# v's block rows in one transfer per pair, whole halo rows without clears, and a new order of the work

## The chip, the cores and the metric

The kernel runs on one core of one Trainium2 chip. The metric is the device time of one execution in microseconds: the median of three runs is 269.15 us (268.91 to 269.34). A core has five engines with queues of their own: TensorE (PE, matmuls), VectorE (DVE), ScalarE (ACT), GpSimd (POOL) and SyncE (SP, which here only issues DMA transfers).

## The reference

Attention over a window of 16 keys to either side plus 24 block summaries (the maximum of k and the mean of v over 32 rows), a value projection with a convolved gate, and a spatial-gating MLP. B, H, S, D are 2, 8, 768, 64; the model width is 512, w_in is 512 x 1024, w_spatial 768 x 768. Cut to what matters:

```python
k_sum = k.reshape(B, H, nb, block, D).max(axis=3)
v_sum = v.reshape(B, H, nb, block, D).mean(axis=3)
mask_l = np.abs(pos[:, None] - pos[None, :]) < window
scores_s = scale * np.einsum('bhsd,bhnd->bhsn', q, k_sum) + np.log(block)
scores_all = np.concatenate([np.where(mask_l, scale * q @ kT, -1e9), scores_s], axis=-1)
attn = softmax(scores_all) @ np.concatenate([v, v_sum], axis=2)        # then x = heads side by side
gate_pre += conv_w[k][None, None, :] * xp[:, k:k + S, :]               # k = 0..4
x = (sigmoid(gate_pre) * (x @ w_val)) @ w_out
u, v = halves of np.maximum(x @ w_in, 0.0)
v_s = np.einsum('ts,bsd->btd', w_spatial, normalised v) + b_spatial[None, :, None]
out = (u * v_s) @ w_out2
```

## The kernel before, in words

Nothing is issued where it is written. Every operation is recorded by the class Planner (record, L100), given a duration by cost (L161), and put in order by plan (L232): a list scheduler that keeps each engine's free time, the slots of 33 tiles of 128 x 1536 floats and of 8 PSUM banks, and a model of the DMA queue. Whatever is ready first goes first; among what is ready within LOOK (L43) of that, the priority decides, which is the place in ORDER (L45). All instructions are then issued by issue (L214), so the trace gives each of them line 230; nearly all tiles in SBUF are called at_u, all PSUM banks at_ps. DMA transfers for SP share 8 semaphores, and the transfer n waits for the landing of transfer n - 8.

ORDER is a list of tokens; each calls the next step of a piece (step, L1276), and a step that needs another calls it first (need, L1286). The pieces that count here:

- mask and hot: the masks and the identity (moves) made by POOL, and awake (L586), nine filler matmuls of moves by moves.
- wout, in1, in0, wval: the loads of w_out, the two halves of w_in, and w_val (split64 L571, load64 L553). The weights are float64 in DRAM; a block of 128 x 512 comes as 512 KB, ACT and DVE (a shift and an or) assemble float32 from it. cw (conv_weights L593) does the same with the 20 KB of convolution weights, which POOL's own queue loads, and POOL copies them to the tile cw.
- wp (w_product L1199): the product of w_out and w_in, 32 matmuls of 128 x 512, first the half n = 1 from in1 and then the half n = 0 from in0, four to a step.
- lk, lq, lv: loads of k, q, v for a pair of heads (L611, L606, L632); kw (windows L616) builds keys in windows and takes the block maximum km on DVE. Pairs 0 to 3 are the first batch, 4 to 7 the second.
- vsum (reduce_v L647) loads v once more in rows and adds up the means on DVE; put (put_vsum L665) sends them by four small SP transfers of 24 x 128 to the partitions 96 to 119, and POOL copies them into the pair's v tile.
- score (L680), at (a_T L712) and pv (L726): for a pair and half of the sequence the 24 score matmuls, the masked maximum on DVE (six operations), the exponential on ACT, the scaling on POOL, six transposes on PE, and 24 matmuls with v; pv also starts the convolution on DVE.
- gate, val0/1, u0/1, v0/1, s0/1, f0/1, ws, out2, r: the projections and the spatial gating, whose products are of 128 x 384 and whose operands are split in two rounded parts by ACT and POOL.

The v tile of a pair holds for each of 12 blocks of 64 queries, and for 2 heads, 120 rows: 32 to 95 are the block itself, 0 to 31 the 16 rows before and the 16 after it, interleaved, 96 to 119 the means. The rows outside the sequence's ends carry weight zero, since the mask puts -1e9 there. In load_v (L632) POOL clears the 32 halo rows of the first and last block, and four SP transfers bring two halves of the 64 rows and the halo rows, shifted by one block.

Of the kernel before, what the change touches and what calls it, by code (L numbers as in the profile page):

```python
# [18 lines left out]
WK = 96  # L19
# [23 lines left out]
LOOK = {"PE": 0, "ACT": 0, "DVE": 0, "POOL": 100, "SP": 200}  # L43

ORDER = """  # L45
    mask in1 hot mask hot wout*2 in1 hot*4 in1 wval wout in1 lk lq hot wval wout lk wp lk wp hot lk kw*2 in0*2 score
    wp lq*2 in0 score kw vsum wp lq in0 vsum score kw score lv score wp*2 at put cw pv lv put score wp at pv lv
    wval*2 put at score*2 wp lv*2 at lk put hot lk at vsum lv at*2 pv*2 kw gate lq lv lq kw wu lq pv*2 val0 wu
    val0*2 lk at wv val0 lv pv wu pv wu wv lk score*2 kw u0 kw u0 gate val0 wv val0 wv vsum u0 put score*2 put lq
    score*4 val0 at u0 v0 at val0 v0 at*2 pv*4 at put v0 at*2 v0*2 put at pv*3 gate pv gate v0 f0 u0 ws*2 val1*4 f0  # L50
    val1 s0 val1 u0 v1 val1 v1 ws u1 v1 ws val1 u0 s0 u1 f1 f0 v1*2 s0 f0 v1 s0 out2 u1 u0 u1 f1 ws f1 s0*2 f1 u1 s0
    s1 out2 f0 s0 s1 s0 out2 ws u1 f0 u1 s1 s0 ws f0 u1 out2 s1*2 s0 s1 s0*2 r*2 s0 r f1*2 s1 r*2 s1 r s1*4 f1 s1*2
    r*6
"""

WIN = 10240 / 3
# [9 lines left out]
class Planner:  # L66
# [86 lines left out]
    @staticmethod  # L153
    def size(ap):
        n = 1
        for _, c in ap.ap[1:]:
            n *= c
        return n

    @staticmethod  # L160
    def cost(o, eng, method, args, kw, ins, outs):  # L161

        size = Planner.size
        n = max(size(x) for x in ins + outs)
        if eng == "PE":
            rhs = args[2]
            cols = size(rhs) if method == "matmul" else args[1].ap[0][1]
            if method == "transpose":
                return 109, None, 0, False
            if rhs.dtype == F32 and outs[0].ap[0][1] > 64:  # L170
                return 4 * cols / 2.4 + 8, None, 0, False
            if rhs.dtype == F32:
                return (4 * cols / (6 if cols > 64 else 4.8) + 8), None, 0, False
            return (cols / 2.4 + 14 if rhs.dtype != BF16 else 200 if cols > 16 else 80), None, 0, False
        psum = any(x.tensor.name.startswith("ps") for x in ins)
        if method == "dma_start":
            run = 4 * min(outs[0].ap[-1][1], ins[0].ap[-1][1]) if ins else 512
            total = 4 * size(outs[0]) * outs[0].ap[0][1]
            parts = outs[0].ap[0][1]
            o.rate = next(k for k in range(16, 0, -1) if parts % k == 0)  # L180
            rate = 130 if run <= 512 else 405 if parts > 96 else 235 if parts > 64 else 380 if parts > 16 else 210
            return (600 if eng == "POOL" else 840 if len(outs[0].ap) > 2 else 600 if parts == 64 else 410), None, total / rate, False
        if eng == "ACT":
            ptr = sum(1 for k in ("bias", "scale") if hasattr(kw.get(k), "ap")) + (method == "mul" and hasattr(args[2], "ap"))
            func = args[2] if method == "activation" else None
            if n <= 4 and outs[0].tensor.name.startswith("ps"):
                return 200, None, 0, False
            table = {AF.Exp: "exp", AF.Tanh: "exp", AF.Prelu: "exp"}.get(func)
            return (n + (61 if psum else 112)) / 1.2 + 93 * ptr + (92 if "accum_out" in kw else 0) + 45 * (func == AF.Prelu), table, 0, False
        sbuf_in = [x for x in ins if not x.tensor.name.startswith("ps")]  # L190
        big = [x for x in sbuf_in if size(x) > 1]
        if eng == "DVE":
            out_psum = outs[0].tensor.name.startswith("ps")
            if method == "memset":
                return n / 0.96, None, 0, False
            one = method in ("tensor_copy", "tensor_scalar") and not psum and not out_psum
            lock = one or len(big) > 1 or n == 1 and not psum
            ptr = sum(1 for x in args[2:5] if hasattr(x, "ap") and size(x) == 1) if method != "tensor_tensor" else 0
            if method == "tensor_reduce" and ins[0].ap[-1][0] > 32:
                n = 1.75 * n  # L200
            per = 8 * n if method == "reciprocal" else n / 2 if one else n
            return (per + 66) / 0.96 + 58 * ptr + 9 * (method == "tensor_tensor_reduce"), None, 0, lock
        if method == "memset":
            return n / 1.2 + 30, None, 0, False
        if method == "affine_select":
            return 450, None, 0, True
        two = len(big) > 1
        if n == 1:
            return 550, None, 0, True
        if two and ins[-1].ap[-1][0] == 0:  # L210
            return 790, None, 0, True
        return (2.45 if two else 1.1 if method == "tensor_copy" else 2.85) * n / 1.2 + 190, None, 0, True
# [237 lines left out]
def tile_kernel(ctx, tc, q, k, v, vn, w_val, conv_w, w_out, w_in, w_sp, b_sp, w_out2, mask_l, mask_r, eye, out):  # L450
    nc = tc.nc
    B, H, S, D = vn.shape
    DM = H * D
    NP = H // 2
    NB = S // QB
# [4 lines left out]
    pe, act, dve, pool, sp = plan.PE, plan.ACT, plan.DVE, plan.POOL, plan.SP  # L460
# [12 lines left out]
    def unit(dt=F32R, n=1536, kind=0):  # L473
        uid[0] += 1
        x = homes.tile([P, 1536], dt, tag="h0", name=f"u{uid[0]}", bufs=1)
        return plan.tile(x, "u", NU, (kind, n))[:, :n]
# [20 lines left out]
    def cst(shape, dt, name):  # L497
        return plan.tile(const.tile(shape, dt, name=name), "const " + name, 1)
# [92 lines left out]
    cw = cst([P, KT, 5], F32, "cw")  # L591
# [11 lines left out]
    QT, KT_, KWT, VW, vsum = {}, {}, {}, {}, {}  # L603
# [28 lines left out]
    def load_v(n):  # L632
        b, p = pairs[n]
        vw = VW[n] = unit(F32).rearrange("p (h j d) -> p h j d", h=2, d=D)
        pool.memset(vw[0:32, :, 0 :: NB - 1, :], 0.0)

        src, dst = v[b, p], vw.rearrange("p h j d -> p (h j d)")
        for h in range(2):
            sp.dma_start(dst[32:WK, h * NB * D : (h + 1) * NB * D], src[:, h * NB * D : (h + 1) * NB * D])
        sp.dma_start(dst[0:32:2, D:], src[48:64, :-D])  # L640
        sp.dma_start(dst[1:32:2, :-D], src[0:16, D:])

    rows = vn.rearrange("b h (n k) d -> (b h n) (k d)", k=32)
    stage, MS, MEAN = Parts(4 * 2 * D, F32), {}, {}
# [599 lines left out]
    def each(n, piece):  # L1244
# [4 lines left out]
    NG = len(ticks)  # L1249
    threads = {  # L1250
        "lk": each(NPR, load_k), "lq": each(NPR, load_q), "mask": load_masks(), "hot": each(9, awake), "kw": each(NPR, windows), "lv": each(NPR, load_v),
        "vsum": each(4, reduce_v), "put": each(NPR, put_vsum), "cw": conv_weights(),
        "score": each(NG, scores), "at": each(NG, a_T), "pv": each(NG, pv), "gate": each(B * NC, gate),
# [122 lines left out]
```

## Time and profile before

| | |
|---|---|
| median of three runs | 269.15 us |
| profiled execution: its own time | 269.44 us |
| profiled execution: span of its instructions | 267.7 us |
| PE busy | 255.7 us, 96% |
| DVE busy | 189.3 us, 71% |
| ACT busy | 158.1 us, 59% |
| POOL busy | 164.1 us, 61% |
| moved by DMA | 31.73 MB, mean 119 GB/s |
| chain that ended last | PE 73%, DMA 17%, SP's queue 3%, POOL 3%, ACT 2%, DVE 1% |

The page comes from one profiled execution. A busy PE is a modelled time, since matmuls are pipelined. The chain is followed back from the last instruction to whatever released each step. In a timeline, consecutive instructions of one kind are put together with a count, and the bracket says how long the engine idled ahead of them and what ended that.

### The profile page before, as it was taken

Reading aid. Unit: us, or ns where it says so; the run is one execution under the profiler, and the core shown is the slowest. Engines: PE = TensorE matmul, PEld = TensorE weight load, DVE = VectorE, ACT = ScalarE, POOL = GpSimd, SP = SyncE. Lnnn points to the kernel's source line nnn. Section 1 sums busy time; section 2 is a strip of 40 time slices with the busy share of each in tenths; the row PEclk is TensorE's granted clock in tenths of the full one; section 3 lists DMA queues with packets and bytes.
Section 4 is the critical chain, followed back from the end, with each engine's and each line's share of the span. In section 5 each row is a group of like instructions: output and inputs, shape, how many; then the busy total and the mean of one; then the engine's idle time right before and its main releaser. Section 6 shows DMA issues by size and latency. Waiting matters only on the chain.

```text
span 267.7 us, 5433 instructions
## 1 busy us (share of the span) xinstructions
PE 255.7 (96%) x1882; PEld 220.7 (82%) x1882; DVE 189.3 (71%) x558; ACT 158.1 (59%) x440; POOL 164.1 (61%) x197
## 2 busy tenths in 40 slices
PE   7799999869999999999999999999999999999995
PEld 5245655459999998988999899889999898889884
DVE  1778998569989995799986868947975547308200
ACT  2459996977998999957570206153445734423311
POOL 6047328475989546991856507586299599684500
PEclk9999999997999999999999999999999999999999
DMA  6999989599761002440000000002004200321122
GB/s 225 390 406 406 400 236 281 156 320 242 291 165 48 2 4 68 147 149 2 5 0 0 0 2 0 0 0 78 4 1 159 43 36 0 115 83 39 42 101 95
DMA packets 11291, 31.73 MB, mean 119 GB/s; under 512 B 1648, under 2 KB 2112, under 8 KB 11264
## 3 DMA queue, kind: packets, MB, share of 16 engines
q1 hardware_dynamic: 11232, 31.37, 34.6%
q8 instruction: 15, 0.25, 0.4%
q14 instruction: 12, 0.10, 0.1%
q0 software_dynamic: 32, 0.02, 0.0%
HBM read 28.14 MB, written 3.15 MB: 117 GB/s over the span
## 4 chain that ended last, share of the span: by engine, by line
PE 73%; DMA 17%; SPq 3%; POOL 3%; ACT 2%; DVE 1%; issue 1%; DVEq 0%; ACTq 0%
PE at_ps L230 73%; DMA at_u<-in_moe_w_out_dram 6%; DMA at_u<-in_k_dram 5%; DMA at_u<-in_q_dram 4%; SPq L230 3%; POOL at_u L230 3%; DMA at_u<-in_moe_w_val_dram 2%; ACT at_u L230 2%; DVE at_u L230 0%; DVE km L230 0%; ACT at_ps L230 0%; DVEq L230 0%; ACTq L230 0%
## 5 line engine op out<-in xcount | busy, mean ns | idle before, releaser
L230 PE MATMUL at_ps<-at_u,at_u 128*128 128x384 f32 (+4 forms) x1752 | 233.5, 323 | 4.0 <-ACT at_u L230 2.1
L230 PEld LDWEIGHTS at_ps<-at_u,at_u 128*128 128x128 f32 (+2 forms) x1752 | 202.4, 190 | 31.6 <-issue 11.6
L230 POOL TENSOR_TENSOR at_u<-at_u,at_u 128x384 fp32r<-128x384 f32 (+2 forms) x83 | 102.8, 1261 | 53.1 <-ACT at_u L230 50.9
L230 ACT CAST at_u<-at_u 128x384 fp32r<-128x384 f32 (+2 forms) x83 | 45.3, 589 | 32.1 <-DVE at_u L230 26.7
L230 ACT COPY at_u<-at_ps 120x384 f32<-120x384 f32 (+3 forms) x61 | 28.0, 500 | 32.9 <-PE at_ps L230 32.5
L230 POOL TENSOR_TENSOR at_u<-at_u,sm 128x360 f32<-128x360 f32 x32 | 25.1, 814 | 18.9 <-ACT at_u L230 9.5
L230 ACT ACTIVATE at_u<-at_u,nm 128x120 f32<-128x120 f32 x96 | 36.5, 389 | 0.3 <-DVE nm L230 0.3
L230 DVE SCALAR_TENSOR_TENSOR at_u<-at_ps,cw,at_u 128x384 f32<-128x384 f32 (+4 forms) x64 | 36.3, 610 | 0.0
L230 DVE TENSOR_TENSOR at_u<-at_ps,at_u 128x384 f32<-128x384 f32 (+1 forms) x36 | 19.8, 554 | 22.7 <-PE at_ps L230 20.7
L230 ACT ACTIVATE at_ps<-at_u 128x512 f32<-128x512 f32 x20 | 13.0, 652 | 20.7 <-DMA at_u<-in_moe_w_out_dram 11.4
L230 DVE CUSTOM_DVE_ANT_0 at_u<-at_ps,mask 128x120 f32<-128x120 f32 x96 | 21.3, 273 | 0.4 <-PE at_ps L230 0.3
L230 DVE TENSOR_TENSOR at_u<-at_u,at_u 128x256 f32<-128x256 f32 (+2 forms) x25 | 19.8, 793 | 1.3 <-PE at_ps L230 0.7
L230 ACT ACTIVATE at_u<-at_ps 128x512 f32<-128x512 f32 x20 | 11.6, 596 | 14.2 <-PE at_ps L230 14.1
L230 POOL COPY at_u<-at_u 128x320 f32<-128x320 f32 (+2 forms) x24 | 18.1, 772 | 1.7 <-DMA at_u<-at_u 1.2
L230 ACT ACTIVATION_READ_ACCUMULATOR at_u<-at_u,nm 128x1 f32 x96 | 18.6, 194 | 0.0
L230 DVE TENSOR_SCALAR at_u<-at_u 128x512 uint32<-128x512 uint32 (+1 forms) x21 | 11.5, 547 | 9.3 <-DMA at_u<-in_moe_w_in_dram 5.6
L230 DVE TENSOR_TENSOR at_u<-at_u 128x384 f32<-128x384 f32 (+5 forms) x31 | 16.2, 534 | 2.6 <-PE at_ps L230 2.6
L230 DVE SCALAR_TENSOR_TENSOR at_u<-at_ps,at_u 128x512 uint32<-128x512 uint32 x20 | 13.8, 690 | 3.8 <-ACT at_ps L230 2.2
L230 PE MATMUL at_ps<-moves,at_u 128*120 128x128 f32 x96 | 12.9, 274 | 2.2 <-DVE at_u L230 2.2
L230 PEld LDWEIGHTS at_ps<-moves,at_u 128*120 128x120 f32 x96 | 11.0, 137 | 4.4 <-DVE at_u L230 2.4
L230 POOL TENSOR_TENSOR va<-va,power 128x1 f32<-128x1 f32 x12 | 8.0, 667 | 10.1 <-DVE va L230 10.1
L230 DVE BATCH_NORM_STATS2 st<-at_u 128x6 f32<-128x512 f32 x12 | 8.2, 688 | 7.3 <-ACT at_u L230 7.3
(38 smaller groups left out, 138.1 us busy)
## 6 DMA issues: line engine op xcount, KB each, us to landing
at_u<-in_moe_w_in_dram SPq DMA_DIRECT2D x8, 512.0 KB, 8.3
at_u<-in_moe_w_out_dram SPq DMA_DIRECT2D x8, 512.0 KB, 6.3
at_u<-in_k_dram SPq DMA_DIRECT2D x8, 384.0 KB, 7.6
at_u<-in_q_dram SPq DMA_DIRECT2D x8, 384.0 KB, 6.9
at_u<-in_vn_dram SPq DMA_DIRECT2D x6, 512.0 KB, 9.1
at_u<-in_v_dram SPq DMA_DIRECT2D x16, 192.0 KB, 5.4
out_dram<-at_u SPq DMA_DIRECT2D x11, 256.0 KB, 2.0
at_u<-in_moe_w_spatial_dram SPq DMA_DIRECT2D x6, 384.0 KB, 3.6
```

The source lines that it names most:

```text
L230: getattr(real, method)(*[home(x) for x in args], **{k: home(x) for k, x in kw.items()})
```

## The change

load_v no longer clears the halo rows. It brings the 64 block rows of both heads by one transfer of 64 x 1536, and the halo rows by two transfers of 16 x 1536 whose source starts one block of a head earlier or later (D elements to the left or to the right), so that the rows are whole; the ends now hold values of neighbouring rows in place of zeros. In Planner.cost the rates of small transfers and one issue time change. ORDER is another list; of it only the first lines are shown.

```diff
 ORDER = """
-    mask in1 hot mask hot wout*2 in1 hot*4 in1 wval wout in1 lk lq hot wval wout lk wp lk wp hot lk kw*2 in0*2 score
-    wp lq*2 in0 score kw vsum wp lq in0 vsum score kw score lv score wp*2 at put cw pv lv put score wp at pv lv
...
+    mask hot wout hot in1*2 hot wout hot*2 lk in1 lq mask hot kw lk wout hot cw wp in0 lq lk score wout in0 in1 hot
+    wp kw lq score kw wp*2 lk kw in0 hot in0 vsum score wp wval at lq lv vsum put at score*2 wv lv wval put pv*2 lv
...
@@ Planner.cost, dma_start
-            rate = 130 if run <= 512 else 405 if parts > 96 else 235 if parts > 64 else 380 if parts > 16 else 210
-            return (600 if eng == "POOL" else 840 if len(outs[0].ap) > 2 else 600 if parts == 64 else 410), None, total / rate, False
+            rate = 130 if run <= 512 else 405 if parts > 96 else 235 if parts > 64 else 260 if parts > 16 else 150
+            return (600 if eng == "POOL" else 980 if parts < 32 and run <= 512 else 840 if len(outs[0].ap) > 2 else 600 if parts == 64 else 410), None, total / rate, False
@@ load_v
         vw = VW[n] = unit(F32).rearrange("p (h j d) -> p h j d", h=2, d=D)
-        pool.memset(vw[0:32, :, 0 :: NB - 1, :], 0.0)
-
         src, dst = v[b, p], vw.rearrange("p h j d -> p (h j d)")
-        for h in range(2):
-            sp.dma_start(dst[32:WK, h * NB * D : (h + 1) * NB * D], src[:, h * NB * D : (h + 1) * NB * D])
-        sp.dma_start(dst[0:32:2, D:], src[48:64, :-D])
-        sp.dma_start(dst[1:32:2, :-D], src[0:16, D:])
+        sp.dma_start(dst[32:WK], src)
+
+        n = 2 * NB * D
+        for t, at in ((0, 48 * n - D), (1, D)):
+            sp.dma_start(dst[t:32:2], bass.AP(src.tensor, src.offset + at, [[n, 16], [1, n]]))
```

What the new list does to the engines, at three places.

The first place is DVE at the very start. An operation TENSOR_SCALAR of 128x512 with the SCALAR_TENSOR_TENSOR behind it assembles one block of a weight; those of 128x20 do the same for the convolution weights. Before:

```order
L230 TENSOR_SCALAR at_u_74_708<-at_u_74_708 128x512
L230 SCALAR_TENSOR_TENSOR at_u_73_771<-at_ps_75_756,at_u_74_708 128x512
L230 TENSOR_SCALAR at_u_79_711<-at_u_79_711 128x512
L230 SCALAR_TENSOR_TENSOR at_u_73_771<-at_ps_80_769,at_u_79_711 128x512
L230 TENSOR_SCALAR at_u_82_718<-at_u_82_718 128x512
L230 SCALAR_TENSOR_TENSOR at_u_73_771<-at_ps_83_781,at_u_82_718 128x512
L230 TENSOR_SCALAR at_u_85_723<-at_u_85_723 128x512
L230 SCALAR_TENSOR_TENSOR at_u_84_793<-at_ps_86_789,at_u_85_723 128x512
```

With the change:

```order
L230 TENSOR_SCALAR at_u_75_708<-at_u_75_708 128x512
L230 SCALAR_TENSOR_TENSOR at_u_74_767<-at_ps_76_754,at_u_75_708 128x512
L230 TENSOR_SCALAR at_u_103_711<-at_u_103_711 128x20
L230 SCALAR_TENSOR_TENSOR at_u_103_711<-at_u_103_711 128x20
L230 TENSOR_SCALAR at_u_79_713<-at_u_79_713 128x512
L230 SCALAR_TENSOR_TENSOR at_u_74_767<-at_ps_80_775,at_u_79_713 128x512
L230 TENSOR_SCALAR at_u_82_717<-at_u_82_717 128x512
L230 SCALAR_TENSOR_TENSOR at_u_74_767<-at_ps_83_785,at_u_82_717 128x512
```

The first block is now one of w_out, and the two operations on the convolution weights stand behind it, ahead of the first block of w_in. They stood far behind these rows before.

The second place is SP's list in the stretch of v. in_v_dram is v by blocks (lv), in_vn_dram v by rows (vsum), the 24x128 transfers are the means (put), and the last in_k_dram rows are k of the pairs 4 and 5. Before, with pair 0's four transfers of v right ahead of the first row:

```order
L230 DMA at_u_204_922<-in_v_dram 64x768 x2
L230 DMA at_u_204_922<-in_v_dram 16x1472 x2
L230 DMA at_u_221_932<-in_v_dram 64x768 x2
L230 DMA at_u_221_932<-in_v_dram 16x1472 x2
L230 DMA at_u_222_1110<-in_moe_w_val_dram 128x1024
L230 DMA at_u_226_1113<-in_moe_w_val_dram 128x1024
L230 DMA at_u_250_1095<-in_v_dram 64x768 x2
L230 DMA at_u_250_1095<-in_v_dram 16x1472 x2
L230 DMA at_u_251_1106<-in_v_dram 64x768 x2
L230 DMA at_u_198_1171<-at_u_155_1104 24x128 x4
L230 DMA at_u_251_1106<-in_v_dram 16x1472 x2
L230 DMA at_u_256_1240<-in_k_dram 128x768 x2
```

With the change, with three transfers each of the pairs 0 and 1 not far ahead:

```order
L230 DMA at_u_202_1041<-in_moe_w_val_dram 128x1024
L230 DMA at_u_213_1055<-in_v_dram 64x1536
L230 DMA at_u_213_1055<-in_v_dram 16x1536 x2
L230 DMA at_u_214_1110<-in_v_dram 64x1536
L230 DMA at_u_214_1110<-in_v_dram 16x1536 x2
L230 DMA at_u_215_1137<-in_moe_w_val_dram 128x1024
L230 DMA at_u_242_1162<-in_q_dram 128x768
L230 DMA at_u_180_1194<-at_u_158_1064 24x128 x4
L230 DMA at_u_247_1228<-in_moe_w_val_dram 128x1024
L230 DMA at_u_251_1232<-in_k_dram 128x768
L230 DMA at_u_242_1162<-in_q_dram 128x768
L230 DMA at_u_251_1232<-in_k_dram 128x768
```

Before, k of the pairs 4 and 5 stands behind five pairs of v with four transfers each; now behind four pairs with three, and behind one q more. The loads of w_val that stood third and sixth in the whole list before now stand among the v rows.

The third place is DVE around the block maxima of the pairs 4 and 5 (TENSOR_REDUCE km). The 128x512 rows are the last blocks of w_val, the rows with cw the convolution of the first pv. Before:

```order
L230 TENSOR_REDUCE km_282<-at_u_256_1240 128x24
L230 TENSOR_REDUCE km_287<-at_u_256_1240 128x24
L230 TENSOR_SCALAR at_u_226_1113<-at_u_226_1113 128x512
L230 SCALAR_TENSOR_TENSOR at_u_226_1113<-at_ps_227_1202,at_u_226_1113 128x512
L230 TENSOR_TENSOR at_u_201_1313<-at_ps_200_1290,at_u_201_1313 128x384
L230 SCALAR_TENSOR_TENSOR at_u_203_1323<-at_ps_200_1290,cw,at_u_203_1323 128x383
L230 SCALAR_TENSOR_TENSOR at_u_203_1323<-at_ps_200_1290,cw,at_u_203_1323 128x382
L230 TENSOR_TENSOR at_u_201_1313<-at_ps_218_1325,at_u_201_1313 128x384
```

With the change:

```order
L230 TENSOR_REDUCE km_289<-at_u_251_1232 128x24
L230 TENSOR_SCALAR at_u_247_1228<-at_u_247_1228 128x512
L230 SCALAR_TENSOR_TENSOR at_u_247_1228<-at_ps_248_1295,at_u_247_1228 128x512
L230 TENSOR_TENSOR at_u_207_1324<-at_ps_206_1300,at_u_207_1324 128x384
L230 SCALAR_TENSOR_TENSOR at_u_209_1332<-at_ps_206_1300,cw,at_u_209_1332 128x383
L230 TENSOR_REDUCE km_305<-at_u_251_1232 128x24
L230 SCALAR_TENSOR_TENSOR at_u_209_1332<-at_ps_206_1300,cw,at_u_209_1332 128x382
L230 TENSOR_TENSOR at_u_207_1324<-at_ps_210_1330,at_u_207_1324 128x384
```

The second maximum moved from ahead of the w_val block to behind it and behind the first two operations of pair 0's pv.

## Rows read from the trace of the kernel before

**Rows 1.** The page, part 1: busy time, share of the span, instructions.

```profile
PE 255.7 (96%) x1882; PEld 220.7 (82%) x1882; DVE 189.3 (71%) x558; ACT 158.1 (59%) x440; POOL 164.1 (61%) x197
```

**Rows 2.** Timeline of PE, 195 to 268 us.

```profile
210.96 53.68 PE L230 MATMUL at_ps<-at_u,at_u 128*128 128x384 f32 x273 [0.60 <-ACT at_u L230]
```

**Rows 3.** Timeline of PE, 0 to 70 us: start, us, engine, line, what, [idle before <-releaser].

```profile
1.87 5.46 PE L230 MATMUL at_ps<-moves 128*128 128x264 f32 x14 [1.87 <-POOL moves L230]
8.25 1.95 PE L230 MATMUL at_ps<-at_u 128*128 128x512 f32 x4 [0.92 <-DVE at_u L230]
...
16.53 0.61 PE L230 MATMUL at_ps<-moves 128*128 128x264 f32 x2
...
22.72 3.70 PE L230 MATMUL at_ps<-at_u 128*128 128x512 f32 x8
26.35 5.85 PE L230 MATMUL at_ps<-at_u,at_u 64*64 64x120 f32 x78
32.77 3.98 PE L230 MATMUL at_ps<-at_u,at_u 64*64 64x120 f32 x30 [0.58 <-DMA at_u<-in_q_dram]
...
47.09 1.88 PE L230 MATMUL at_ps<-at_u,at_u 64*64 64x120 f32 x44 [0.90 <-ACT at_u L230]
49.61 3.70 PE L230 MATMUL at_ps<-at_u,at_u 128*128 128x512 f32 x8 [0.63 <-ACT at_u L230]
53.50 0.99 PE L230 MATMUL at_ps<-at_u,at_u 120*64 120x64 f32 x24 [0.19 <-POOL at_u L230]
...
59.28 1.20 PE L230 MATMUL at_ps<-moves,at_u 128*120 128x128 f32 x9 [2.18 <-DVE at_u L230]
```

**Rows 4.** Windows: busy us (count) of PE, PEld, DVE, ACT, POOL, PEclk, DMA share, GB/s.

```profile
60.00:66.00 6.00, 6.00 (x107) 5.76 (x106) 5.96 (x16) 5.28 (x13) 3.02 (x4) 0.72 1.01 246
62.00:64.00 2.00, 2.00 (x44) 2.00 (x42) 2.00 (x6) 1.75 (x7) 0.00 (x0) 0.50 1.02 251
```

**Rows 5.** Groups by line and form, POOL: count, busy us, mean ns.

```profile
L230 POOL MEMSET at_u<- 32x256 f32 x8 | 2.4, 302 | 0.1
```

**Rows 6.** Timeline of SP's queue, 26 to 60 us.

```profile
26.89 14.18 SPq L230 DMA_DIRECT2D at_u<-in_v_dram  x12
```

**Rows 7.** The page, part 2: GB/s in 40 slices of 6.7 us.

```profile
GB/s 225 390 406 406 400 236 281 156 320 242 291 165 48 2 4 68 147 149 2 5 0 0 0 2 0 0 0 78 4 1 159 43 36 0 115 83 39 42 101 95
```

**Rows 8.** Timeline of DVE, 40 to 64 us.

```profile
43.94 0.81 DVE L230 SCALAR_TENSOR_TENSOR at_u<-at_u 128x20 uint32<-128x20 uint32 x1
...
55.22 0.95 DVE L230 TENSOR_REDUCE km<-at_u 128x24 f32<-128x768 f32 x1 [4.34 <-DMA at_u<-in_k_dram]
...
58.53 0.69 DVE L230 SCALAR_TENSOR_TENSOR at_u<-at_ps,at_u 128x512 uint32<-128x512 uint32 x1
```

**Rows 9.** The tile of v's loads: SP's issues, min/median/max ns.

```profile
L230 SPq DMA_DIRECT2D at_u<-in_v_dram x32: 517/536/1367, 26.9 to 74.2; - x32
```

**Rows 10.** Timeline of POOL, 0 to 30 us.

```profile
1.77 0.15 POOL L230 MEMSET mask<- 128x72 f32 x1
```

**Rows 11.** DMA issues: count, KB each, median us to landing.

```profile
at_u<-in_moe_conv_w_dram POOLq DMA_DIRECT2D x1, 20.0 KB, 5.6
```

**Rows 12.** Timeline of DVE, 0 to 13 us.

```profile
10.53 0.69 DVE L230 SCALAR_TENSOR_TENSOR at_u<-at_ps,at_u 128x512 uint32<-128x512 uint32 x1 [0.32 <-ACT at_ps L230]
11.14 0.42 DVE L230 TENSOR_SCALAR at_u<-at_u 128x512 uint32<-128x512 uint32 x1
11.77 0.69 DVE L230 SCALAR_TENSOR_TENSOR at_u<-at_ps,at_u 128x512 uint32<-128x512 uint32 x1 [0.21 <-ACT at_ps L230]
```

**Rows 13.** Groups by line and form, PE and DVE.

```profile
L230 DVE CUSTOM_DVE_ANT_0 at_u<-at_ps,mask 128x120 f32<-128x120 f32 x96 | 21.3, 273 | 0.4 <-PE at_ps L230 0.3
...
L230 PE MATMUL at_ps<-at_u,at_u 64*64 64x120 f32 x384 | 17.7, 303 | 1.5 <-ACT at_u L230 0.9 <-DMA at_u<-in_q_dram 0.6
...
L230 PE MATMUL at_ps<-moves,at_u 128*120 128x128 f32 x96 | 12.9, 274 | 2.2 <-DVE at_u L230 2.2
...
L230 DVE TENSOR_REDUCE km<-at_u 128x24 f32<-128x768 f32 x8 | 7.4, 948 | 5.7 <-DMA at_u<-in_k_dram 5.6
```

More of the change, by code (lines that the diff above doesn't have):

```diff
@@ L45 @@
 ORDER = """
-    mask in1 hot mask hot wout*2 in1 hot*4 in1 wval wout in1 lk lq hot wval wout lk wp lk wp hot lk kw*2 in0*2 score
-    wp lq*2 in0 score kw vsum wp lq in0 vsum score kw score lv score wp*2 at put cw pv lv put score wp at pv lv
[L48 to L53, printed above, removed]
+    mask hot wout hot in1*2 hot wout hot*2 lk in1 lq mask hot kw lk wout hot cw wp in0 lq lk score wout in0 in1 hot
+    wp kw lq score kw wp*2 lk kw in0 hot in0 vsum score wp wval at lq lv vsum put at score*2 wv lv wval put pv*2 lv
+    put lv wval wp at score pv score put lq at wval lk pv wu gate score wp lq wp at lk at lq lk val0 at val0 kw pv
+    val0 at val0 lv wu kw lk kw wv score pv*3 wu lv gate lq score wu vsum u0 kw u0 val0 u0 vsum wv*2 lv at val0
+    put*2 val0 score*6 lv v0 at val0 at v0 u0 at pv*3 at put at v0*2 at*2 pv*3 put pv gate pv ws gate u0 v0*2 val1*2
+    ws f0 val1*2 f0 val1*2 s0 v1 out2 v1 u0 v1 val1*2 u1 ws u1 v1 f1 u1 v1 u1 s1 v1 f0 s0 f1 f0 s1 u1*2 f1 s1 s0 s1
+    s0 f1 u1 f1 ws s0*2 u1 s0 ws s0 s1*2 u0 ws f0*2 s0 out2 s0 out2*2 u0 r s0 s1*2 r s0 f0 ws s0 r s0 r s1*2 f1 s1
+    f1 s1 r s1 r*4 s1 r*3
 """
```

## The prediction

> **What bounds the kernel now.** I read the page's first part, then the timeline of TensorE (PE) with the idle time that ends each stretch, then for each idle time the timeline of the engine it names, and SP's issues last. TensorE is busy for 255.7 of 267.7 us [rows 1], so all its idle time is 12.0 us, and only the places where that stands can give anything. From about 60 us on there is one wait, of 0.60 us [rows 2]; the rest lies ahead. The reader is to see three groups in the timeline [rows 3]: the start (1.87 us until the filler matrix is made, and 0.92 until VectorE, DVE, has assembled the first w_in block), four waits between 32 and 54 us (0.58 + 0.90 + 0.63 + 0.19 = 2.30 us), and 2.18 us ahead of the stretch at 59.28. The last has a tail: the mean granted clock of the 6 us behind it is 0.72, and 0.50 in their middle [rows 4], the lower of the two levels (1.2 GHz). That costs 6 x 0.28 = 1.7 us.
>
> **Time base.** The profiled execution took 269.44 us, 0.29 over the median of 269.15. The sum is made against 269.44, and 0.29 is taken off at the end. About 0.2% (0.54 us) is what a measurement of this kernel can tell from no change.
>
> **The change, part by part.**
>
> *The clears.* Eight POOL memsets of 0.302 us go [rows 5], 2.4 us in all. The transfer of v into the same tile comes behind each of them and hides it, and no engine waits for POOL's clears in the trace: I cost them at nothing. Without that cover they would be worth 2.4 us at most.
>
> *v's transfers.* Two halves of 192 KB become one of 384 KB, and two of 92 KB become two of 96 KB: 576 KB a pair in three issues instead of 568 KB in four, so eight of SP's issues go. In the v stretch SP spent 14.18 us on 12 issues, 1.18 us each [rows 6], and the rate falls from 400 GB/s to 236, 281 and 156 there [rows 7]: the queue did not wait for bytes. No row shows a transfer of 16 x 1536 or 64 x 1536. By bytes at 400 GB/s a pair takes 1.5 us, by issues at 1.18 us it takes 3.5; I take the issues, since v was served at their pace.
>
> *k of the second batch.* It stands in SP's list behind 20 v issues before and behind 12 now, with nearly the same bytes ahead (16.6 and 16.4 MB, added up from the list) and one q load more among them. Before, the first pair's k (pair 4) lands at 55.2, when DVE has idled for 4.34 us [rows 8]. Eight issues of 0.54 us (the median of v's issues [rows 9]) less 0.97 us for the q (0.39 MB at 406 GB/s [rows 7]) are 3.3 us; half of that is my lower value. So it lands between 52 and 53.5.
>
> *The conv weights.* Their POOL transfer moves from the middle of the start to right behind the second memset of the mask at 1.77 us [rows 10], and their two DVE operations come to stand between the first w_out block and the first w_in block. The transfer took 5.6 us to land [rows 11], in a queue as full as the one at the start, so it lands at 1.92 + 5.6 = 7.5. The two operations take some 0.95 (the longer alone 0.81 [rows 8]), the block behind them 1.1 [rows 12], and the first product begins at about 9.75 in place of 8.25: TensorE idles for 2.4 us instead of 0.92. That is 1.5 us; the bounds are nothing (it has landed before DVE comes to it) and 7.1 us (it takes twice 5.6 us).
>
> *The products.* DVE is then the bound: eight blocks at 1.24 us from one to the next [rows 12], three block maxima of k at 0.95, twelve score operations at 0.22 (21.3 / 96) [rows 13], and an estimated 0.6 for four small ones, are 16.0 us behind 9.6. So the last four products of the first half start at 25.6 and, with 3.63 us for four [rows 3], end at 29.25. Before, they end at 26.35, but two scores (1.11 us each: 17.7 over 16 [rows 13]) and a filler (0.61 [rows 3]) fewer have been done by then: like for like, 29.2. So the late start is paid for by the order that follows. From there to the first output matmuls at 53.50, before loses 2.30 us to the four waits. In the new order the work to that point, four sets of 3.63, five scores and four and a half transposes (0.81 each: 12.9 over 16 [rows 13]), runs to 53.0, with 1.2 us of transposes and one filler more behind it than before. **First term: 2.30 - 0.05 = 2.2 us gained**, between 0.8 (the two longest of these waits come back, 0.90 and 0.63) and 3.7 (no late start).
>
> *Around the block maxima.* Before, the maxima of pairs 4 and 5 both stand ahead of the last w_val block and of the first pair's convolution on DVE. That block's second operation ends at 58.53 + 0.69 = 59.22 [rows 8] and frees the bank that the transposes at 59.28 wait for. Now one maximum stands ahead of the block, the other behind it and two operations of the convolution, and k is there 1.7 to 3.3 us sooner: with k at 53.5, the maximum and the block are done by 55.7, before TensorE ran out of work (59.28 - 2.18 = 57.1). The 2.18 us go, and with them the 1.7 us of the lower clock. Something else is late next: ACT, which now serves two w_val blocks, the scaling of the last products and the exponentials of the scores in the same stretch. I charge it two waits of the size of its largest, 0.90 [rows 3]. **Second term: 3.9 - 1.8 = 2.1 us**, between 0 and 3.9.
>
> *The rest.* Behind 60 us TensorE has no gap but one, and the same products in another order cost nothing while the other engines keep ahead. The nearest price for a stall is the 0.60 us [rows 2]; I take none, and allow 1 us either way.
>
> **Sum.** 269.44 - 2.2 - 2.1 = 265.14; less 0.29 it is 264.85, said as **264.9 us**.
>
> **The rivals.**
>
> *The conv weights land early.* For it: they are only 20 KB. Against it: 5.6 us [rows 11]. The first product would start at 8.25 as before, DVE's chain and with it TensorE come 1.5 us sooner, and the time is 264.85 - 1.5 = 263.4. The Trainium skill, "DMA: Bandwidth & Descriptors", section "Anatomy of one DMA — SWDGE (gpsimd) path", gives a transfer on POOL's path about 2.0 us plus its bytes over 436 GB/s: by that, an estimate, it lands at about 4.0, and this rival holds. The trace disagrees, with 5.6 us for the very same transfer. Chance 0.17.
>
> *k as late as before.* The wide rows of v may be served no faster than the narrow ones, and then the first maximum waits as it did. The second term is nothing: 264.85 + 2.1 = 267.0. Against it: eight issues fewer ahead of k. Chance 0.15.
>
> *Given back.* The new order also moves POOL's subtractions of rounded values, w_spatial's among them, and the gating's products; POOL, busy for 61% of the span [rows 1], can be late for the gating, and 4.3 us of waits in TensorE's full stretch undo the gain. The same comes out if the change does not do what it says and v's rows are no sooner there in sum. 269.1, no difference. Against it: one wait only behind 60 us. Chance 0.10.
>
> *Slower: the clock falls at the start.* Before, 2.18 us idle were followed by a stretch at the lower clock [rows 3, 4]. The new idle time at 7.3 us is as long, 2.4 us, and TensorE has no slack from 25 us on. One such stretch costs up to 1.7 us; one or two eat into the gain, and from the third it decides: 264.85 + 3 x 1.7 = 269.95. For it: the same length of idle time. Against it: until 25 us DVE sets the pace, so that part of a slow stretch is hidden. Chance 0.13.
>
> **How the numbers follow.** Forecast 0.45 (its own range 263.0 to 267.0, from the two terms at half the way to their ends), early weights 0.17, late k 0.15, given back 0.10, slower 0.13. Faster by over 0.2% are the first three, 0.77; the same 0.10; slower 0.13. The range goes from 262.7 (early weights, and 0.7 of the 1 us of the later part) to 269.2 (the gain given back), and leaves out the slower case and the ends.
>
> **What would show it.** Right: the first 128 x 512 matmul between 9.5 and 10 us, after some 2.4 us idle that DVE ends; the four waits between 32 and 54 us mostly gone; the first maximum of the second batch begun before 54 us; no window near 60 us under 0.9 of the clock. Wrong: the first product at 8.3 (early weights); 2 us idle near 57 us with a slow stretch behind it (late k); idle time of TensorE beyond 80 us (given back); a granted clock of 0.5 between 10 and 30 us (slower).

## The result, and the profile after

The changed kernel takes 265.98 us (median of nine runs, 264.81 to 267.58), the kernel before in the same comparison 268.91 (nine runs, 268.36 to 269.34): a ratio of 0.990, 95% interval 0.987 to 0.9929. That is 2.9 us gained where 4.3 were forecast (264.9 us, range 262.7 to 269.2). The profiled execution took 267.57 us, 1.87 less than that of before (269.44), and it is one of the longest of the nine. Its page, part 1 and the summary of the chain:

```profile
PE 257.4 (97%) x1882; PEld 220.8 (83%) x1882; DVE 183.5 (69%) x558; ACT 157.9 (59%) x440; POOL 162.1 (61%) x189
...
PE 91%; DVE 4%; DMA 3%; issue 0%; POOL 0%; ACT 0%; DVEq 0%; POOLq 0%
```

TensorE's idle time fell from 12.0 [rows 1] to 8.4 us, and TensorE was busy 1.7 us longer for the same matmuls. The chain is now nearly all TensorE, with 3% for the load of the convolution weights. The timeline of TensorE, the rows that answer to [rows 2, 3]:

```profile
1.87 5.83 PE L230 MATMUL at_ps<-moves 128*128 128x264 f32 x14 [1.87 <-POOL moves L230]
10.94 6.73 PE L230 MATMUL at_ps<-at_u 128*128 128x512 f32 x8 [3.23 <-DVE at_u L230]
...
56.77 0.92 PE L230 MATMUL at_ps<-at_u,at_u 120*64 120x64 f32 x24
...
99.24 2.32 PE L230 MATMUL at_ps<-at_u,at_u 128*128 128x384 f32 x12 [0.20 <-DVE at_u L230]
```

The 1.87, 3.23 and 0.20 us are all that is left of its waits, apart from the tail of 3.1 us behind its last matmul. None stands between 32 and 60 us, where before had four and the 2.18 us. In exchange the first product starts at 10.94 instead of 8.25, behind 3.23 us of idle time. What stands behind it shows in the windows of 2 us (busy us and count of PE, PEld, DVE, ACT, POOL, then the granted clock, the DMA share, GB/s), which answer to [rows 4]:

```profile
10.00:12.00 2.00, 1.06 (x2) 0.58 (x3) 1.80 (x4) 1.80 (x3) 0.19 (x2) 0.57 1.03 416
12.00:14.00 2.00, 2.00 (x4) 0.93 (x3) 2.00 (x4) 0.64 (x1) 1.19 (x3) 0.50 1.04 419
14.00:16.00 2.00, 2.00 (x3) 0.67 (x2) 0.07 (x1) 1.33 (x2) 0.82 (x3) 0.50 1.03 408
16.00:18.00 2.00, 2.00 (x5) 0.76 (x3) 0.24 (x1) 0.13 (x1) 0.00 (x0) 0.72 1.04 406
```

The stretch at the lower clock has not gone: it has moved from 60 us to the start, and in this execution it is twice as long. DVE shows why the start is late, and what the slow products do to it:

```profile
4.82 0.69 DVE L230 SCALAR_TENSOR_TENSOR at_u<-at_ps,at_u 128x512 uint32<-128x512 uint32 x1 [0.26 <-ACT at_ps L230]
9.20 0.18 DVE L230 TENSOR_SCALAR at_u<-at_u 128x20 uint32<-128x20 uint32 x1 [3.69 <-DMA at_u<-in_moe_conv_w_dram]
...
10.10 0.69 DVE L230 SCALAR_TENSOR_TENSOR at_u<-at_ps,at_u 128x512 uint32<-128x512 uint32 x1
...
17.76 0.69 DVE L230 SCALAR_TENSOR_TENSOR at_u<-at_ps,at_u 128x512 uint32<-128x512 uint32 x1 [3.70 <-PE at_ps L230]
```

DVE has its first w_out block done at 5.5 us, and its two operations on the convolution weights, next in its order, wait 3.69 us for their load. Later, with a weight block in hand, it waits 3.70 us for TensorE and its slow products. The transfer's own row, which answers to [rows 11]:

```profile
at_u<-in_moe_conv_w_dram POOLq DMA_DIRECT2D x1, 20.0 KB, 7.3
```

### The profile page after: what moved, and what is told of

It reads as the page before. It is cut to its first block, busy times and chain, and to the rows that moved or that the text cites. A ratio compares the mean times of both kernels' runs of the same rounds, so it can differ in the third digit from the quotient of the medians.

```text
span 265.8 us, 5404 instructions
## 1 busy us (share of the span) xinstructions
PE 257.4 (97%) x1882; PEld 220.8 (83%) x1882; DVE 183.5 (69%) x558; ACT 157.9 (59%) x440; POOL 162.1 (61%) x189
## 4 chain that ended last, share of the span: by engine, by line
PE 91%; DVE 4%; DMA 3%; issue 0%; POOL 0%; ACT 0%; DVEq 0%; POOLq 0%
PE at_ps L230 91%; DVE at_u L230 4%; DMA at_u<-in_moe_conv_w_dram 3%; POOL mask L230 0%; DVE nm L230 0%; ACT at_u L230 0%; POOL moves L230 0%; POOL power L230 0%; DVE sm L230 0%; DVEq L230 0%; POOLq L230 0%; POOLq L1358 0%
## 5 line engine op out<-in xcount | busy, mean ns | idle before, releaser
L230 DVE SCALAR_TENSOR_TENSOR at_u<-at_ps,cw,at_u 128x384 f32<-128x384 f32 (+3 forms) x64 | 36.3, 605 | 0.0
L230 POOL COPY at_u<-at_u 128x320 f32<-128x320 f32 (+2 forms) x24 | 17.5, 742 | 0.9
L230 DVE TENSOR_TENSOR at_u<-at_u,at_u 128x256 f32<-128x256 f32 (+2 forms) x25 | 17.1, 688 | 0.1
L230 DVE TENSOR_SCALAR at_u<-at_u 128x512 uint32<-128x512 uint32 (+1 forms) x21 | 10.1, 487 | 9.5 <-DMA at_u<-in_moe_w_out_dram 5.9
L230 DVE TENSOR_TENSOR at_u<-at_u 128x384 f32<-128x384 f32 (+5 forms) x31 | 15.5, 512 | 0.1
L230 PE MATMUL at_ps<-at_u 128*128 128x512 f32 x16 | 10.7, 820 | 3.2 <-DVE at_u L230 3.2
L230 DVE SCALAR_TENSOR_TENSOR at_u<-at_u,at_u 128x384 f32<-128x384 f32 x16 | 13.1, 857 | 0.1
```

Source lines behind the costliest of these rows:

```text
L230: getattr(real, method)(*[home(x) for x in args], **{k: home(x) for k, x in kw.items()})
```

## Where the 1.87 us come from

From the two timelines the time can be cut at the first output matmuls (53.50 before [rows 3], 56.77 after). Up to there the new order has done more work: 9 of the transposes (1.2 us) and one filler (0.6) that before still had to do. So the start **lost** 56.77 - 53.50 - 1.8 = 1.5 us. (TensorE idled less there, 5.1 us against 6.2, but at the lower clock the first eight instructions of 128 x 512 took 6.73 us, against 3.63 in experiment 1 at the full clock.) Behind it, 267.7 - 53.50 = 214.2 us were left before and 265.8 - 56.77 = 209.0 are now, 5.2 less, of which the 1.8 are work done earlier: the rest **gained** 3.4 us. 3.4 - 1.5 = 1.9, the difference of the spans. These are terms of two single executions, of which the later one is a long one; between the medians the gain is 2.9.

The nine runs of the changed kernel stand in three groups, and the mean granted clock of each run tells them apart: 264.81 and 265.03 us at 1.000, 265.75 to 266.15 at 0.992 to 0.994, 267.35 to 267.58 at 0.987. In the kernel before the mean clock does not tell short runs from long ones: of its 47 runs beside the experiments, the 14 with a mean clock of 0.998 or more have a median of 268.98 us, the 33 others 268.88. The experiments ask what makes the groups, what the late weights cost, and which part of the change the 3.4 us are.

## The experiments

All keep the planned lists and edit them by a small function that takes named operations out of the list and puts them back ahead of another one, or by a branch where the list is issued. The lines of a diff are of Planner.issue. A ratio is to the kernel before, run on the same chip with it; the experiments ran on three chips, so where two of them differ by little the intervals of their ratios decide.

### 1. The convolution weights later

```diff
+        order = self.shift(order, lambda o: o.piece[0] == "cw" and o.call[1] != "dma_start",
+                           lambda o: o.piece == ("wp", 3))
```

> The changed kernel, with only the four operations on the convolution weights behind their load (one on ACT, two on DVE, the copy on POOL) moved from ahead of the first w_in block to right ahead of the last four products of the n = 1 half; the load itself stays at the front. Theory (the late conv weights hold up DVE, TensorE's idle 3.23 us behind them brings its granted clock down): the first product starts by 7.9 us, right behind the fillers or at most 0.5 us later, no window of 2 us between 8 and 20 us shows a clock under 0.9, all runs lie together, and the time is 262.0 to 264.0 us. Rival (the blocks of w_in are late anyway, the weights only hide it): first product at 9.5 us or later, 265 to 267 us. Second rival (DVE's later chain sets the end of the half, whatever the start): first product by 7.9, but the last four products of the half start at 28 us or later as now, and 265 to 266 us.

264.42 us (263.81 to 264.71), ratio 0.9834 (0.9811 to 0.9858), clear of the changed kernel's interval. TensorE:

```profile
7.25 3.63 PE L238 MATMUL at_ps<-at_u 128*128 128x512 f32 x8
12.41 4.92 PE L238 MATMUL at_ps<-at_u,at_u 128*128 128x512 f32 x32 [1.52 <-DVE at_u L238]
...
52.22 0.92 PE L238 MATMUL at_ps<-at_u,at_u 120*64 120x64 f32 x24
...
56.13 0.43 PE L238 MATMUL at_ps<-moves,at_u 128*120 128x128 f32 x2 [0.52 <-DVE at_u L238]
```

The first product starts at 7.25, right behind the fillers, no window shows a lower clock and no run a mean under 0.998. The time is 0.4 us above the expected range: the theory holds, with some less in it than hoped. Cut as above, 53.50 - 52.22 + 1.8 = 3.1 us are now gained at the start and 214.2 - 1.8 - (262.0 - 52.22) = 2.6 behind it: what the late weights had hidden from view is a first DVE wait of 0.52 us at 56.13 (and, within the start, the one of 1.52 at 12.41).

### 2 and 7. Fillers in the gap

```diff
+            if o.piece == ("hot", 6):
+                for i in range(4):        # 9 in the second of the two
+                    getattr(real, method)(*[home(x) for x in args], **{k: home(x) for k, x in kw.items()})
```

> The changed kernel with the seventh filler matmul issued four times more, so that TensorE works through the idle 3.23 us (four times 0.8 us) while the conv weights stay where they are. Theory (the idle time brings the clock down, and the clock makes the difference between the runs of 264.9, 266.0 and 267.5 us): the first product still starts at about 11 us, the clock shows 1.00 there, DVE's wait of 3.70 us for TensorE at 14 us shrinks by more than half, and all runs lie within 0.5 us at about 264.9. Rival (the clock falls for the sparse products behind, not for the idle time): the median stays at about 266.0 and the runs stay apart by over 2 us. Second rival (the fillers only cost): 266.5 or more.

> The changed kernel with the seventh filler issued nine times more instead of four, so that TensorE is busy from 1.87 us to within 0.7 us of the first product at 10.9 us. Theory (the idle time brings the clock down): no window under 0.95 of the clock between 8 and 20 us, all runs within 0.8 us of one another, median 264.3 to 264.9. Rival (sparse products bring it down): some runs at 266 or more with the clock at 0.5 behind 11 us, median over 265.

With four fillers: 264.66 us (264.32 to 266.62), ratio 0.9865 (0.9833 to 0.9896). Four of six runs lie at 264.3 to 264.9 with a clock of 0.998 or more; a fifth took 266.62 at 0.999, which the clock does not explain. In the profiled one (266.09 us, 0.994) the fillers ran faster than I had reckoned, 2.12 us of idle time were left ahead of the first product, and the lower clock is there for one stretch:

```profile
10.80 5.37 PE L233 MATMUL at_ps<-at_u 128*128 128x512 f32 x8 [2.12 <-DVE at_u L233]
```

```profile
12.00:14.00 2.00, 2.00 (x4) 0.71 (x3) 1.96 (x4) 0.64 (x1) 1.14 (x3) 0.52 1.05 422
14.00:16.00 2.00, 2.00 (x4) 0.81 (x3) 0.00 (x0) 1.38 (x2) 0.81 (x3) 0.63 1.02 406
```

With nine, no idle time is left ahead of the first product, which comes at 11.69. 264.97 us (264.51 to 265.35; 264.3 to 264.9 was expected), ratio 0.9848 (0.9816 to 0.988), every run at a clock of 0.999 or 1.000:

```profile
12.00:14.00 2.00, 2.00 (x6) 0.92 (x5) 2.00 (x5) 0.64 (x1) 1.32 (x4) 1.00 1.03 416
14.00:16.00 2.00, 2.00 (x5) 0.60 (x4) 0.86 (x3) 1.17 (x2) 0.68 (x3) 1.00 1.02 408
```

So it is the idle time that brings the clock down, and not the products behind it, which are the same. The kernel with its first product as late as before, and 0.75 us later still, is 1.0 us faster in the median when TensorE works through the wait, and its runs lie together (the intervals of the two ratios overlap by 0.001). DVE's later wait for TensorE falls from 3.70 to 1.14 us. With the weights out of the way instead the median is another 0.55 lower (264.42), which the overlapping intervals do not tell from nothing. The first expectation, that four would do, missed.

### 11. The load of the weights first

```diff
+        order = self.shift(order, lambda o: o.piece[0] == "cw" and o.call[1] == "dma_start", lambda o: True)
```

> The changed kernel, with the load of the convolution weights issued as POOL's first instruction after the constants, some 1.1 us sooner and level with SP's first transfer; nothing else moves, and POOL's fillers' matrix comes some 0.7 us later for it. Theory (it lands late because of the weights that are queued ahead of it on the DMA engines): it lands 5 us or less after its issue, DVE goes on by 6.5 us, the first product starts by 8.3 us, and the time is 264.0 to 265.2 us. Rival (the load takes its 7.3 us whatever is queued): it lands at about 8 us, the first product starts at about 9.7 us, the clock still falls in some runs, and the time is 265.2 to 266.5 us.

264.62 us (263.67 to 266.47), ratio 0.9846 (0.9805 to 0.9887).

```profile
at_u<-in_moe_conv_w_dram POOLq DMA_DIRECT2D x1, 20.0 KB, 4.9
```

```profile
6.16 0.18 DVE L238 TENSOR_SCALAR at_u<-at_u 128x20 uint32<-128x20 uint32 x1 [0.59 <-DMA at_u<-in_moe_conv_w_dram]
```

```profile
3.12 5.79 PE L238 MATMUL at_ps<-moves 128*128 128x264 f32 x14 [3.12 <-POOL moves L238]
8.76 3.60 PE L238 MATMUL at_ps<-at_u 128*128 128x512 f32 x8
```

Issued at 1.25 instead of 1.87 us the same 20 KB land after 4.9 instead of 7.3 us, at 6.16 instead of 9.20: 0.6 us of lead gives 3.0. So the time that the load takes hangs on when it is issued among the others, and not on its 20 KB. One block of 512 KB fewer is issued ahead of it (two at 0.74 and 1.19 us, where three were); at the 248 to 377 GB/s of the changed kernel's windows between 2 and 8 us that is 1.4 to 2.1 us, an estimate, and how the rest of the 2.4 us comes about is open. The first product starts at 8.76, 0.5 later than expected since the fillers start 1.25 us later too, and right behind them, so that the clock stays up.

### 3 and 6. v loaded as before, in the new order

Each load of v is issued as in the kernel before (the clear, two transfers of 64 x 768, two of 16 x 1472), at the place of the new ones.

```diff
+            if o.piece[0] == "lv":
+                dst, src = home(args[0]), args[1]
...
+                    self.POOL.real.memset(clear, 0.0)
+                    for h in range(2):
+                        real.dma_start(dst[:, h * 768 : (h + 1) * 768], src[:, h * 768 : (h + 1) * 768])
...
+                    real.dma_start(dst[:, cut : cut + n - 64], src[:, cut : cut + n - 64])
+                continue
```

> The changed kernel with its order kept row by row, but each load of v issued as before: the POOL clear, two transfers of 64 x 768 and two of 16 x 1472 where the three new ones stand. Theory (the gain comes from the order around the block maxima, and k has some 4 us of slack now, since DVE reaches it at 57.5 us): within 0.5 us of the changed kernel. Rival (the gain comes from the wide transfers, which let k and the later v arrive): 1.2 us or more slower than the changed kernel, with TensorE or DVE waiting for a DMA between 50 and 70 us.

> The first experiment with v loaded as before (POOL clear, two 64 x 768 and two 16 x 1472 transfers), the order kept. It repeats the third experiment where no lower clock at the start blurs it, and with DVE reaching the first maximum at 53.7 us instead of 57.5. Theory (in the new order v's transfers have slack): within 0.5 us of the first experiment. Rival (four more issues ahead of k, at about 1 us each, make the maximum wait): DVE waits 1 us or more for k near 54 us, and the time is 265.2 us or more.

In the changed kernel: 266.45 us (265.99 to 267.79), ratio 0.9919 (0.9893 to 0.9946). In experiment 1, where the start does not blur it: 264.85 (263.68 to 265.89), ratio 0.985 (0.9818 to 0.9881). Both are within 0.5 us of their counterparts, on the slower side, and the intervals overlap: in the new order v's wide transfers and the missing clears are worth nothing that these runs can tell. The waits of SP's queue between 40 and 60 us in the changed kernel show where the saved issues go (us in all, times, longest):

```profile
SPq L230 <- ACT at_u L230: 3.6, 1, 3.6
```

```profile
43.23 0.33 SPq L230 DMA_DIRECT2D at_u<-in_q_dram  x1
47.52 3.24 SPq L230 DMA_DIRECT2D at_u<-at_u  x4
50.87 0.44 SPq L230 DMA_DIRECT2D at_u<-in_moe_w_val_dram  x1
51.37 0.42 SPq L230 DMA_DIRECT2D at_u<-in_k_dram  x1
```

SP idles from 43.56 to 47.52 us, 3.6 us of it until ACT has scaled the means that the four small transfers carry. Only then come the last w_val block and k. What v's issues saved is spent there; with v loaded as before, in experiment 3, the same wait is still there, and 2.1 us long. Without the late start it is shorter, 0.9 us in experiment 1, and k is issued at 48.21 us there and at 48.86 in experiment 6; in both DVE finds k landed when it comes to it, at 53.75 and 52.87.

### 4. The new transfers of v in the old order

The kernel before, its list kept, each pair of v brought by the three wide transfers and without the clear (the branch is the mirror image of the one above).

> The kernel before with its order kept row by row, but each load of v issued as in the change: no POOL clear, one transfer of 64 x 1536 and two of 16 x 1536. Here the first block maximum of the second batch stands ahead of the last w_val block and waits for k, behind 15 issues of v where 20 were. Theory: k lands 1 to 4 us sooner (51 to 54 us instead of 55.2), the wait of 2.18 us before the stretch at 59.28 shrinks by at least 1 us, and the time is 266.0 to 268.4 us, the more so if the lower clock behind it goes too. Rival (transfers of v cost nothing where they stand): within 0.3 us of the kernel before, 268.9.

267.53 us (266.53 to 267.94), ratio 0.9947 (0.9927 to 0.9966): 1.2 us. DVE and TensorE:

```profile
53.91 0.95 DVE L244 TENSOR_REDUCE km<-at_u 128x24 f32<-128x768 f32 x1 [3.31 <-DMA at_u<-in_k_dram]
```

```profile
47.09 8.02 PE L244 MATMUL at_ps<-at_u,at_u 64*64 64x120 f32 x76 [1.70 <-ACT at_u L244]
...
58.31 1.20 PE L244 MATMUL at_ps<-moves,at_u 128*120 128x128 f32 x9 [0.59 <-DVE at_u L244]
```

k is there 1.3 us sooner (53.91 instead of 55.2) and the 2.18 us shrink to 0.59, as the theory said. In the old order the transfers do count, because the maxima wait for k there. But only 1.3 us sooner, not the 1.7 to 3.3 that I had reckoned, and a wait for ACT at 47.09 grew from 0.90 to 1.70. The lower clock has not gone either: in this execution it stands behind that wait, with 0.63 from 48 to 50 us and 0.52 from 50 to 52, and four of the eight runs have a mean of 0.994.

### 5 and 8. The block maxima

Experiment 5 takes experiment 1 and puts pair 5's maximum back ahead of the last w_val block. Experiment 8 takes the kernel before and moves both maxima behind that block and two operations of the convolution.

```diff
 # 5
+        order = self.shift(order, lambda o: o.piece == ("kw", 5) and o.call[1] == "tensor_reduce",
+                           lambda o: o.piece == ("wval", 3) and o.eng == "DVE")
 # 8
+        order = self.shift(order, lambda o: o.piece in (("kw", 4), ("kw", 5)) and o.call[1] == "tensor_reduce",
+                           lambda o: o.piece == ("pv", 0) and o.eng == "DVE" and o.call[2][0].ap[-1][1] == 382)
```

> The first experiment (conv weights later) with the block maximum of pair 5 put back ahead of the last w_val block on DVE, right behind that of pair 4, as in the kernel before. Theory (what stands ahead of that block on DVE delays the bank that TensorE waits for): the wait of 0.52 us at 56.13 us in the first experiment grows by about the maximum's 0.95 us, and the time is 264.8 to 265.6 us, 0.4 to 1.2 over the first experiment. Rival (the maxima's place does not matter once k is there): within 0.3 us of the first experiment, 264.4.

> The kernel before, with nothing changed but both block maxima (pairs 4 and 5) moved on DVE behind the last w_val block and the first two operations of the first pair's convolution. Theory (the second term of the prediction is this order alone): the wait of 2.18 us ahead of the stretch at 59.28 goes or falls under 0.6 us, the lower clock behind it goes, and the time is 265.3 to 267.2 us. Rival (something else is late next, ACT or k itself): a wait of more than 1.5 us within 5 us of the same place, and 267.8 us or more.

Experiment 5: nine runs from 264.27 to 269.44 us, median 267.26. Without the two longest, the profiled one (268.54) among them, the median is 266.88 and the ratio 0.9908 (0.9875 to 0.994): 2.5 us over experiment 1 in the median, 2.0 by the ratios, for one DVE operation of 0.95 us at another place.

```profile
54.04 1.80 DVE L239 TENSOR_REDUCE km<-at_u 128x24 f32<-128x768 f32 x2
```

```profile
57.76 0.43 PE L239 MATMUL at_ps<-moves,at_u 128*120 128x128 f32 x2 [1.86 <-DVE at_u L239]
```

```profile
58.00:60.00 2.00, 2.00 (x28) 1.68 (x27) 1.96 (x5) 1.43 (x4) 1.92 (x2) 0.65 1.06 307
60.00:62.00 2.00, 2.00 (x8) 1.94 (x7) 2.00 (x5) 1.81 (x5) 2.00 (x4) 0.50 1.02 328
```

The wait grows from 0.52 to 1.86 us, more than the 0.95 expected, and with it the lower clock is back. Seven of the nine runs show a mean clock of 0.992 or 0.994, the two longest and five of the seven others; of the two at 1.000 one took 264.27, as experiment 1, the other 267.75. In the profiled execution the picture of before [rows 3, 4] comes back with this one move. The expected range was too low; it had left out the clock.

Experiment 8: 267.25 us (266.47 to 268.88), ratio 0.9951 (0.9927 to 0.9975), 1.7 us under the kernel before in the median. The 2.18 us are gone, but others come up behind:

```profile
61.97 0.54 PE L239 MATMUL at_ps<-moves,at_u 128*120 128x128 f32 x3 [0.95 <-POOL at_u L239]
...
74.93 0.62 PE L239 MATMUL at_ps<-at_u,at_u 128*128 128x384 f32 x2 [0.90 <-ACT at_u L239]
```

Both sides were half right: the wait goes, and 0.95 for POOL, 0.90 and 0.27 for ACT take most of its place. The profiled execution shows no lower clock, but four of the twelve runs have a mean of 0.994, and these lie at 268.36 to 268.88 us, the other eight at 266.47 to 267.83.

### 9 and 10. Combinations

Experiment 9 is experiment 1 with both maxima behind; experiment 10 is the kernel before with the new transfers of v and both maxima behind.

> The first experiment (conv weights later) with both block maxima moved behind the last w_val block and the first two operations of pair 0's convolution on DVE. If DVE's path to the last w_val block is still what TensorE waits for at 56 us, the wait of 0.52 us goes, nothing brings the clock down, and the time is 263.5 to 264.3 us. Rival (a wait moves on, as POOL and ACT waited in the kernel before with the maxima behind: 0.95, 0.90 and 0.27 us): 264.4 us or more, with a wait of over 0.5 us between 57 and 80 us.

> The kernel before in its own order, with v's three wide transfers and both maxima behind the last w_val block, so all of the change but the new list. Theory (in the old order the two cures answer to the same wait, k late and maxima ahead, and the conv weights and the loads at the start are the list's own): little more than the maxima alone, 266.3 to 267.3 us, so that the new list without its late conv weights (264.4) is worth 2 us or more beside them. Rival (the two add up): 265.0 to 266.0 us.

Experiment 9: 265.3 us (264.87 to 267.94), ratio 0.9897 (0.9849 to 0.9945).

```profile
56.35 0.43 PE L240 MATMUL at_ps<-moves,at_u 128*120 128x128 f32 x2 [0.52 <-DVE at_u L240]
...
65.16 2.01 PE L240 MATMUL at_ps<-at_u,at_u 128*128 128x384 f32 x10 [0.72 <-DVE at_u L240]
```

The rival held: the 0.52 us stay, so it is not the maximum that they wait for, and 0.72 us appear at 65.16. No better place for the maxima than the new order's is shown. Experiment 10: 266.45 (265.04 to 268.12), ratio 0.9911 (0.9877 to 0.9945), in the theory's range, though the interval does not rule out that the two add up. The new transfers and the maxima without the list give about 2.4 us; the whole change without its mistake at the start (experiment 1) gives 4.3.

## Why the prediction was right, and where not

The time lay in the range and the direction was right. But the terms were not the measured ones, and that errors of both signs met near the forecast is luck; so is it that the two runs in which the clock held, 264.81 and 265.03, are its 264.9. Of the four signs of being right two came (the four waits gone, no slow window near 60 us) and two did not (the first product at 10.94 and not by 10, the first maximum at 57.54 and not before 54), and one of the signs of being wrong did come, the clock of 0.5 between 10 and 30 us.

*The conv weights.* The step failed in its size. They landed at 9.20, not 7.5: 7.3 us behind their issue, not the 5.6 of [rows 11]. The first product came at 10.94, not 9.75. The 5.6 us I took were from a full queue too, and yet not a bound. The rival of an early landing was wrong by 5 us; the Trainium skill's figure ("DMA: Bandwidth & Descriptors", "Anatomy of one DMA — SWDGE (gpsimd) path": some 2.0 us and the bytes) is met by no run here, with 4.9 and 7.3 us measured. Experiment 11 shows that its place among the other loads sets its time.

*The products (first term).* "DVE is then the bound" failed: with the clock down it was TensorE, which held DVE up for 3.70 us. DVE's chain was also one block short: nine blocks of 128 x 512, and not eight, stand in the timeline between the convolution weights and these products, 1.24 us more by the sum's own price, so that the term would have been 1.0 and not 2.2. The last four products of the half could start at 30.46 us (29.77 + 0.69, DVE's last block), not at 25.6. Forecast 2.2 gained, measured 1.5 lost. With the late weights out of the way (experiment 1) the term is 3.1 us, near the upper bound of 3.7 that I gave for no late start. The four waits between 32 and 54 us did go. The list of waits at the start had left out one, of 1.07 us, which the timeline of before shows behind the first products:

```profile
11.28 1.12 PE L230 MATMUL at_ps<-at_u,at_u 128*128 128x512 f32 x2 [1.07 <-DVE at_u L230]
```

The sum is not changed by it, since it goes by the times at which the products end.

*The clock at the start.* I had this as the rival that ends on the slower side, with 0.13. Its mechanism was real, in seven of nine runs, and absent in all fifteen of experiments 1, 7 and 11, which leave no idle time there or 1.52 us at most; only its price was smaller than needed to decide: about 1.1 us in the median run and 2.6 in the longest (against the runs at 1.000), one or two stretches, where three would have been needed. The Trainium skill ("TensorE: Matmul & The Clock Gate", Part 1, "What's actually happening") says of the slow stretch at the start of a kernel that its length differs from run to run of the same kernel. Here the stretch stands behind an idle time and not at the very start, and its length differs too: the means of 1.000, 0.993 and 0.987 say so.

*k and v.* The step "it lands between 52 and 53.5" did not hold: k is issued at 51.37 against 52.07, only 0.7 us sooner, since SP waits for the means ahead of it. The profile after does not show when it landed, for DVE came to it only at 57.54 and did not wait; with the 3.1 us that it took before from issue to landing it is 54.5, an estimate. The late start has its part in that. In experiment 1, without it:

```profile
48.21 0.42 SPq L238 DMA_DIRECT2D at_u<-in_k_dram  x1
```

```profile
53.75 0.91 DVE L238 TENSOR_REDUCE km<-at_u 128x24 f32<-128x768 f32 x1
```

DVE takes k at 53.75 without a wait, so it had landed by then. Eight issues fewer are no time gained where the queue then waits for something else.

*Around the maxima (second term).* Forecast 2.1, measured 3.4 (2.6 in experiment 1). In the profiled executions the 2.18 us and the slow stretch behind them went in full, and the 1.8 us charged for ACT did not come; the late start is not the reason, for in experiment 1 no wait for ACT comes either, and only DVE's 0.52 us. But the 1.7 us for the slow stretch are not shown as a price of the kernel before: its runs at a mean clock of 0.998 or more are no shorter than the others (268.98 and 268.88 us), so a longer time elsewhere must stand against it in them, and no trace shows such a run. Experiments 5 and 8 show that the places of the maxima alone make and unmake the wait. In the first, 0.95 us on DVE became 2.0 to 2.5 us of the time, and in most of its runs a slow stretch comes with it.

*Clears and the rest.* Nothing, as said: the one wait left behind 60 us is the 0.20.

## What to carry to other kernels

When an operation moves to the front of an in-order engine, look at what its input waits for, and do not price a small load there by its size, or by the time that it took at another place in the queue; put the load first or its users late. Count with a wait of TensorE the stretch at the lower clock that can follow it, look in the runs at either mean clock whether that stretch costs time, and take the wait away or fill it with matmuls that nobody needs. And before counting issues saved as time, look at what the queue waits for next.

The lowest median is that of experiment 1, the changed kernel with the users of the convolution weights out of the way: 264.42 us, 1.7% under the kernel before. Experiment 11 with its load first (264.62) is not told apart from it.

## What had not been expected of the hardware

A load of 20 KB on POOL's queue needed 7.3 us when issued at 1.87 us and 4.9 us when issued at 1.25. The granted clock fell in the traces behind idle times of TensorE of 1.70 us (experiment 4), 1.86 (experiment 5), 2.12 (experiment 2), 2.18 (before), 2.84 (experiment 3) and 3.23 us. By the mean clocks this happened in one of six runs of experiment 2, in seven of nine of the changed kernel and in all six of experiment 3; in experiments 1 and 9, whose traces have idle times of 1.52 and 1.64 us at the start, in none of eleven.

Open is the rest of the spread, and why the kernel before takes no less time in its runs at a full clock. Some runs at a full clock are long: 266.62 in experiment 2, 267.75 in experiment 5, 267.18 and 267.94 in experiment 9. No trace shows one of these runs, and the cause of the second wait in experiment 5's profile, 1.65 us for DVE at 214.65, is not known.
